# Zeros for the pooled keys made by the transposes, one-hots moved to GpSimd, and unread matmuls at the start

## The chip, the cores and the metric

One core of a Trainium2 chip runs the whole kernel. The metric is the device time of one execution in microseconds (us). Ten runs of the kernel before had a median of 254.6 us, from 253.77 to 255.77. The profile comes from one further execution.

## What is computed

Two stages follow each other. The first is attention with pooled keys and values: 8 batches of 8 heads, 576 positions, 64 dims. The mean over 8 neighbouring positions turns k and v into 72 pooled rows per head. The second routes each of the 4608 tokens (512 wide) through one of 8 experts, chosen by an input `domain_id`.

```python
k_p = k.reshape(B, H, Sp, pool, D).mean(axis=3)          # pool = 8, Sp = 72
v_p = v.reshape(B, H, Sp, pool, D).mean(axis=3)
scores = scale * np.matmul(q, k_p.transpose(0, 1, 3, 2))
attn = softmax(scores)
x = np.matmul(attn, v_p)                                  # -> (4608, 512)
for e in range(E):                                        # 8 experts
    mask = domain_id == e
    out[mask] = np.maximum(x[mask] @ w1[e], 0.0) @ w2[e]
```

All inputs are float32 in HBM. The kernel works in float16 and accumulates in float32.

## The kernel before

**Order.** The instruction order of every engine is written out by hand: the code issues instructions engine by engine in the order in which its functions are called (`tc.manual_schedule()`), and a list `plan` of (due time, unit) pairs, sorted by due time, says in which order the units of the attention stage are called. The due times are only an order, not microseconds. Each engine then works its instructions off in that order and waits where data or a buffer is missing.

**Loads.** Attention works on pairs of batches, `pr` = 0 to 3. For each pair, `load_pair` (line L108) brings k, q and v into SBUF, each with one transfer of 1152 KB as float16 (pair 0's q in two parts). All of them are issued by GpSimd and go, converted from float32 on the way, through one DMA queue (q0 of the profile) in the order of issue: k, q, v of pair 0, then of pair 1, 2, 3, then the first expert's w1. The tiles have two buffers each, so a load of pair 2 is issued once pair 0's tile is read, and so on.

**Head.** While the first k is loaded, VectorE zeroes four tiles (L118: the two gather buffers `xg`; L123: the two `kz` tiles), then builds index constants and, with a few small matmuls (L175, L183, L187), the expert number of each token. `rank_mm` (L216) and `rank_post` (L223 to L248) count tokens per expert, `slot_post` and `perm_prep` turn this into a slot per token.

**Pooled keys.** `kp_units(pr)` pools k: 16 matmuls with an identity (L424), accumulated in PSUM and copied to `kps`. Then `turn` transposes each of the 9 groups of `kps` into two halves of partitions (L432). The halves are copied (L417 on VectorE, L415 on ScalarE) into `kz`, where partitions 0 to 63 hold the keys for even positions and partitions 64 to 127 those for odd positions. The other half of each stays at the zeros written once at the start, so that a score matmul over 128 partitions (L507) picks one parity.

**The rest of a pair.** `qt_units` transposes q (L489, L491, L493), `vp_units` pools v (L455 to L476), `sc_unit` makes scores and their exponentials (L507, L509), `av_unit` multiplies with v and divides (L526 to L531) into `x_sb`. Three `av_unit`s fill a tile of 384 KB that `x_write` (L545) sends to the DRAM tensor `x_lin` on the queue of SyncE (q1 of the profile). `x_rows` holds the writes of pairs 0 and 1 back behind a one-row transfer `gate` (L550) that reads the last v tile, so none of them starts before the last v has landed. There are 12 such writes, nine for pairs 0 to 2.

**One-hots.** `perm_units(pr)` builds, for the 9 token columns of a pair, the one-hot rows `op` of the slot's low 7 bits (L345 on VectorE, three columns at a time), `eq` of its block (L352 on VectorE), and `vc` from `eq` (L359 on GpSimd). `perm_mm` (L371) multiplies them on TensorE. The result is the list of rows that each expert gathers.

**Experts.** After the writes of pairs 0 to 2, GpSimd gathers rows of `x_lin` by indirect DMA (L589), first three blocks for expert 0, then w2 of expert 0 (tag `q`, L583), three blocks for expert 1, and w1 and w2 of expert 1 (tags `v`, `k`). TensorE transposes the gathered rows (L603), makes the hidden layer (L639) and the output (L655). Results leave by indirect DMA (L664).

Of the kernel before, what the change touches and what calls it, by code (L numbers as in the profile page):

```python
# [7 lines left out]
F32 = mybir.dt.float32  # L8
F16 = mybir.dt.float16
I32 = mybir.dt.int32  # L10
AFT = mybir.ActivationFunctionType
# [10 lines left out]
NC_ = 9  # L22
# [17 lines left out]
def kernel(  # L40
# [27 lines left out]
    def wide():  # L68
        return ps.tile([128, 8, 128], F32, tag="wide", bufs=1, name="wide")
# [41 lines left out]
    with tc.manual_schedule():  # L111
# [2 lines left out]
        nc.sync.dma_start(dom64[:], moe_domain_id.bitcast(I32).rearrange(  # L114
            "(p s two) -> p s two", p=64, two=2))
        xg = [per.tile([128, NBL, HD], F16, name="xg%d" % i) for i in range(2)]
        for t in xg:
            nc.vector.memzero(t[:].rearrange("p j d -> p (j d)"))  # L118
        kt, vt, qt_ = {}, {}, {}

        kz = [wk.tile([128, 2, 16, 72], F16, tag="kz", bufs=2, name="kz") for i in range(2)]
        for t in kz:
            nc.vector.memzero(t[:].rearrange("p a b c -> p (a b c)"))  # L123
        kt[0] = load_pair(k, 0, "k")
        qt_[0] = load_pair(q, 0, "q", (0, 48, 72))

# [15 lines left out]

        iota_f = rt.tile([128, 128], F32, name="iota_f")
        nc.vector.tensor_copy(iota_f[:], iota_row[:])
        iota_h = const.tile([128, 128], F16, name="iota_h")
        nc.vector.tensor_copy(iota_h[:], iota_row[:])
        col_f = const.tile([128, 1], F32, name="col_f")
        nc.vector.tensor_copy(col_f[:], iota_col[:])
        ident = const.tile([128, 128], F16, name="ident")
# [31 lines left out]
        for cc in range(NC_):  # L181
            if cc <= 4:
                nc.tensor.matmul(Rv[:, :, cc, :], selA[:, 128 * cc:128 * cc + 128], domT[:, :, 0, :],  # L183
                                 start=True, stop=(cc < 4), skip_group_check=True)
            if cc >= 4:
                c0 = 128 * (cc - 4)
                nc.tensor.matmul(Rv[:, :, cc, :], selB[:, c0:c0 + 128], domT[:, :, 1, :],  # L187
                                 start=(cc > 4), stop=True, skip_group_check=True)
        g_i = rt.tile([128, 1], I32, name="g_i")
        nc.vector.tensor_scalar(out=g_i[:], in0=iota_col[:], scalar1=7, scalar2=None,  # L190
                                op0=ALU.bitwise_and)
# [14 lines left out]
        blk_h = blk_i = c0 = gap = mrow = mt = nblk_f = nblk_i = nov_f = od = ork = orun = ovf = ovf_h = pos_h = pos_i = rank = rk = run_ = slot_i = slotf = tmp = None  # L206
# [5 lines left out]
        def rank_mm():  # L212
            nonlocal rk
            rk = small(), small()
            for t, w in zip(rk, (Lm, ones)):
                nc.tensor.matmul(t[:, 0:E * NCH], w[:], oh[:].rearrange("p e c -> p (e c)"),  # L216
                                 start=True, stop=True)
# [75 lines left out]
            return v.units  # L293

        def perm_prep():
            nonlocal blk_h, blk_i, pos_h, pos_i
# [7 lines left out]
            pos_h = const.tile([128, NCH], F16, name="pos_h")  # L304
            nc.vector.tensor_copy(pos_h[:], pos_i[:])
            blk_h = const.tile([128, NCH], F16, name="blk_h")
            nc.vector.tensor_copy(blk_h[:], blk_i[:])

        def token_of(pool, row, n, v=nc.vector):

# [26 lines left out]
        def perm_units(pr):  # L337
            cs = slice(NC_ * pr, NC_ * pr + NC_)
            box = {}

            def op(i):
                if i == 0:
                    box["op"] = rt.tile([128, NC_, 128], F16, tag="op", bufs=2, name="op")
                c0 = NC_ * pr + 3 * i
                nc.vector.tensor_tensor(box["op"][:, 3 * i:3 * i + 3, :],  # L345
                                        iota_h[:].unsqueeze(1).to_broadcast([128, 3, 128]),
                                        pos_h[:, c0:c0 + 3].unsqueeze(2).to_broadcast([128, 3, 128]),
                                        op=ALU.is_equal)

            def pick():  # L350
                eq = rt.tile([128, NC_, NBLK], F16, tag="eq", bufs=2, name="eq")
                nc.vector.tensor_tensor(eq[:], iota_h[:, 0:NBLK].unsqueeze(1).to_broadcast([128, NC_, NBLK]),  # L352
                                        blk_h[:, cs].unsqueeze(2).to_broadcast([128, NC_, NBLK]),
                                        op=ALU.is_equal)
# [50 lines left out]
        def kp_units(pr):  # L405
            s = st.setdefault(pr, {})
            kk = kt[pr][:].rearrange("p (w t) d -> p t w d", t=8)
            kps = wk.tile([128, 9, D], F16, tag="kps", bufs=1, name="kps")
            kpT = kz[pr % 2]
            s["kpT"] = kpT  # L410
            box = {}

            def evac(dst, src, act):
                if act:
                    nc.scalar.activation(dst, src, AFT.Copy)  # L415
                else:
                    nc.vector.tensor_copy(dst, src)  # L417

            def pool(w0, w1, t0):
                if t0 == 0:  # L420
                    box[w0] = small()
                pv = box[w0][:, 0:64 * (w1 - w0)].rearrange("p (w d) -> p w d", d=64)
                for t in range(t0, t0 + 4):
                    nc.tensor.matmul(pv, ident[:], kk[:, t, w0:w1, :], start=(t == 0), stop=(t == 7))  # L424
# [267 lines left out]
        for pr in range(NP):  # L692
            t0 = 16.0 * pr
            for h in range(16):
                plan.append((t0 + h, -1, lambda pr=pr, h=h: sc_unit(pr, h)))

            if pr + 1 < NP:
                at = [8.6 + 1.78 * j for j in range(NC_)]
                if pr == NP - 2:
                    at[4:] = [16.1, 17.1, 18.2, 19.3, 20.4]  # L700
            else:
                at = [9.2, 10.7, 12.2, 13.7, 16.0, 16.4, 17.0, 17.6, 18.2]
            for j in range(NC_):
                plan.append((t0 + at[j], len(plan), lambda pr=pr, j=j: av_unit(pr, j)))
            k0, k1 = (2.6, 6.6) if pr < NP - 1 else (0.5, 6.5)
            put([lambda pr=pr, i=i: run(vp_units_(pr, i)) for i in range(11)], t0 + k0, t0 + k1)
            if pr + 1 < NP:
                put([lambda pr=pr, i=i: run(kp_units_(pr + 1, i)) for i in range(6)], t0 + 7.5, t0 + 11.0)
# [197 lines left out]
```

## Time and profile before

| | us |
|---|---|
| median of 10 runs | 254.6 |
| lowest and highest of them | 253.77, 255.77 |
| the profiled execution: its time | 256.01 |
| the profiled execution: its span, first to last instruction | 254.3 |
| TensorE busy in the span | 220.3 (87%) |
| VectorE busy | 126.5 (50%) |
| ScalarE busy | 94.4 (37%) |
| GpSimd busy | 117.2 (46%) |
| mean granted TensorE clock | 0.981 |

"PE" is TensorE's matmuls, "PEld" its weight loads, "DVE" VectorE, "ACT" ScalarE, "POOL" GpSimd, "SP" SyncE. A name like L424 is the line of the kernel before. The time between the span and the execution's time, 1.7 us here, lies outside of the first and last instruction. All positions such as "at 80.43" are microseconds from the span's start.

### The profile page before, as it was taken

To read this page: it belongs to the slowest core of one execution; us is meant where nothing else is said; L and a number is where in the kernel's file an instruction comes from. 1 tells how busy PE (TensorE), PEld (TensorE's weight loads), DVE (VectorE), ACT (ScalarE), POOL (GpSimd) and SP (SyncE) were. 2 spreads that over 40 slices of the span, in tenths; PEclk is the share of its full clock that TensorE was granted. 3 is DMA by queue.
4 is the path that set the end of the run, shared out by engine and by line. 5 is a ranking of instruction groups with operands and counts; after the bars stand their busy time and mean duration, and the time that the engine had idled before them with its cause. 6 is when DMAs were issued, how large, how long until landed. Compare 5 with 4: busy or idle time off the path is not lost.

```text
span 254.3 us, 4896 instructions
## 1 busy us (share of the span) xinstructions
PE 220.3 (87%) x1979; PEld 145.9 (57%) x1979; DVE 126.5 (50%) x283; ACT 94.4 (37%) x159; POOL 117.2 (46%) x157
## 2 busy tenths in 40 slices
PE   0287779999987769799989999999999999999990
PEld 0156667777766445445645755756755656656640
DVE  7856889686779752233242433332343332343320
ACT  2037777888785805122311321312302312303210
POOL 8000613130000382276856776676676767653042
PEclk9999999999999968999999999999999999999997
DMA  6999999999999279998989979969969969942032
GB/s 107 207 222 210 223 216 212 220 216 211 215 254 409 89 156 239 238 276 169 182 255 147 253 205 151 245 208 163 248 210 177 249 178 206 248 170 106 1 113 91
DMA packets 21372, 50.20 MB, mean 197 GB/s; under 512 B 2334, under 2 KB 10592, under 8 KB 19938
## 3 DMA queue, kind: packets, MB, share of 16 engines
q0 software_dynamic: 19536, 45.10, 83.1%
q1 hardware_dynamic: 1810, 4.76, 4.8%
q8 instruction: 16, 0.26, 0.4%
q14 instruction: 10, 0.08, 0.1%
HBM read 67.15 MB, written 15.20 MB: 324 GB/s over the span
## 4 chain that ended last, share of the span: by engine, by line
PE 53%; DVE 13%; issue 10%; DMA 9%; ACT 7%; POOL 5%; POOLq 1%; DVEq 0%; ACTq 0%
PE big L639 16%; PE small L655 14%; DMA v<-in_moe_w_dram 6%; PE wide L639 6%; PE wide L655 3%; ACT at L509 3%; DVE x_sb L531 3%; PE small L424 3%; POOL out_dram L664 3%; PE turn L603 3%; DVE qT L493 2%; DMA x_lin<-x_sb 2%; PE small L489 2%; PE big L507 2%; POOL xg L589 2%
## 5 line engine op out<-in xcount | busy, mean ns | idle before, releaser
L589 POOL DMA_INDIRECT xg<-x_lin,xrow x40 | 41.5, 1038 | 48.5 <-DVE tok L100 33.4
L664 POOL DMA_INDIRECT out_dram<-y,tok x40 | 40.2, 1006 | 44.9 <-DVE y L660 19.4
L655 PEld LDWEIGHTS <-hT 128*128 128x128 f16 x272 | 25.9, 98 | 26.6
L645 DVE TENSOR_SCALAR hT<-big 128x640 f16<-128x640 f32 (+1 forms) x24 | 17.4, 725 | 33.4 <-PE big L639 23.9
L509 ACT ACTIVATE at<-big 72x576 f16<-72x576 f32 x45 | 28.3, 646 | 8.4 <-PE big L507 7.3
L662 ACT ACTIVATE y<-small 128x512 f32<-128x512 f32 x16 | 9.6, 597 | 50.2 <-PE small L655 48.0
L643 ACT ACTIVATE hT<-big 128x640 f16<-128x640 f32 (+1 forms) x24 | 15.0, 623 | 31.7 <-PE big L639 31.7
L660 DVE COPY y<-small 128x512 f32<-128x512 f32 x16 | 11.1, 691 | 29.6 <-PE small L655 26.5
L639 PEld LDWEIGHTS <-v 128*128 128x128 f16 x192 | 18.7, 98 | 10.3 <-issue 1.8
L639 PEld LDWEIGHTS <-k 128*128 128x128 f16 x192 | 19.1, 100 | 8.9 <-issue 1.7
L639 PE MATMUL big<-xT,v 128*128 128x320 f16 (+2 forms) x144 | 21.8, 299 | 1.5 <-DVE hT L645 0.9
L604 DVE COPY xT<-turn 128x1024 f16<-128x1024 f16 (+1 forms) x24 | 14.3, 598 | 16.8 <-PE turn L603 13.8
L639 PE MATMUL big<-xT,k 128*128 128x320 f16 (+2 forms) x140 | 21.9, 307 | 0.0
L507 PE MATMUL big<-qT,kz 128*72 128x288 f16 x90 | 18.3, 287 | 2.5 <-DVE qT L493 1.1
L655 PE MATMUL small<-q,hT 128*128 128x512 f16 x80 | 18.6, 379 | 0.0
L655 PE MATMUL small<-k,hT 128*128 128x512 f16 x80 | 18.4, 379 | 0.0
L526 PEld LDWEIGHTS <-at 72*128 72x128 f16 (+1 forms) x320 | 14.8, 104 | 5.9 <-issue 2.6
L531 DVE TENSOR_TENSOR x_sb<-big,rcp 128x512 f16<-128x512 f32 x22 | 15.2, 692 | 0.8
L639 PEld LDWEIGHTS <-q 128*128 128x128 f16 x128 | 12.5, 98 | 5.2
L603 PEld LDWEIGHTS <-xg 128*128 128x128 f16 x160 | 10.9, 99 | 7.8 <-DMA xg<-x_lin,xrow 2.3
L603 PE MATMUL turn<-ident,xg 128*128 128x128 f16 x160 | 13.7, 224 | 1.8 <-DMA xg<-x_lin,xrow 1.6
L655 PE MATMUL small<-v,hT 128*128 128x512 f16 x64 | 14.8, 379 | 0.0
(152 smaller groups left out, 336.4 us busy)
## 6 DMA issues: line engine op xcount, KB each, us to landing
k<-in_moe_w_dram POOLq DMA_DIRECT2D x6, 1024.0 KB
q<-in_moe_w_dram POOLq DMA_DIRECT2D x5, 1024.0 KB
v<-in_moe_w_dram POOLq DMA_DIRECT2D x5, 1024.0 KB
k<-in_k_dram POOLq DMA_DIRECT2D x4, 1152.0 KB
v<-in_v_dram POOLq DMA_DIRECT2D x4, 1152.0 KB
x_lin<-x_sb SPq DMA_DIRECT2D x12, 384.0 KB, 6.9
q<-in_q_dram POOLq DMA_DIRECT2D x3, 1152.0 KB
q<-in_q_dram POOLq DMA_DIRECT2D x1, 768.0 KB
```

The lines of the kernel that those rows point to most:

```text
L507: nc.tensor.matmul(p[0:72, par, 0:288], s["kpT"][:, par, bh, :], s["qT"][:, :, 8 * bh:8 * bh + 8], start=True, stop=True)
L509: nc.scalar.activation(at[0:72, bh % 8, :].rearrange("p (a c) -> p a c", a=2), p[0:72, :, 0:288], AFT.Exp, scale=1.0 / 64.0)
L526: nc.tensor.matmul(pv[r0:r0 + z - a, h, 0:65], s["at", bt][0:72, h, a:z], s["vp"][0:72, 8 * bt + h, :], start=True, stop=True, skip_group_ ...
L531: nc.vector.tensor_tensor(out=x_sb.rearrange("p (h d) -> p h d", d=D), in0=pv[:, :, 0:64], in1=rcp[:].unsqueeze(2).to_broadcast([128, 8, D ...
L589: i = nc.gpsimd.indirect_dma_start(out=xg[e % 2][:, j, :], out_offset=None, in_=x_lin[0:rows, :], in_offset=bass.IndirectOffsetOnAxis(ap=x ...
L603: nc.tensor.transpose(p[:, j - a, kk, :], xg[e % 2][:, j, 128 * kk:128 * kk + 128], ident[:])
L604: nc.vector.tensor_copy(xts[e][:, :, 128 * a:128 * z].rearrange("p k (j c) -> p j k c", c=128), p[:, 0:z - a])
L639: nc.tensor.matmul(p[:, a, 0:m], w1[:, kk, 128 * fi:128 * fi + 128], xT[:, kk, s0 + m * a:s0 + m * a + m], start=(kk == 0), stop=(kk == 3))
L643: nc.scalar.activation(dst, p[:, 0:nh, 0:m], AFT.Relu)
L645: nc.vector.tensor_scalar(out=dst, in0=p[:, 0:nh, 0:m], scalar1=0.0, scalar2=None, op0=ALU.max)
L655: nc.tensor.matmul(p, hT[:, fi, 128 * j:128 * j + 128], w2[:, fi, :], start=(fi == 0), stop=(fi == 7))
L664: i = nc.gpsimd.indirect_dma_start(out=out, out_offset=bass.IndirectOffsetOnAxis(ap=orig[0][:, bl:bl + 1], axis=0), in_=y[:], in_offset=No ...
```

## The change

- Only the first gather buffer is still zeroed by VectorE. ScalarE copies those zeros into the second one, and into `kps`, which is now one permanent tile with 64 zero columns on either side of the pooled keys.
- `turn` transposes 128 columns of `kps` at a time, the keys and 64 zeros before or behind them. The zero rows of `kz` therefore come out of the transposes, and all 128 partitions are copied at once: three copies per pair (groups 0 to 3, 4 to 7, 8), on VectorE except for one of pair 0 on ScalarE. `kz` is no longer zeroed beforehand.
- The one-hots `op` are built on GpSimd, one column per instruction, 36 instructions in all. `eq` reads float32 instead of float16.
- `warm(n)` issues n matmuls of 512 columns on zeros, whose result nobody reads: 6 before the first transposes, 4 after the small matmuls, 3 after `rank_mm`.

In the changed kernel GpSimd's queue holds, behind the load of q of pair 2: 9 `op`, 2 `vc`, 9 `op`, load v of pair 2, 2 `vc`, 6 `op`, load k of pair 3, 3 `op`, 2 `vc`, load q of pair 3, 9 `op`, load v of pair 3, 2 `vc`, load w1 of expert 0, and then the gathers.

```diff
-        for t in xg:
-            nc.vector.memzero(t[:].rearrange("p j d -> p (j d)"))
+        kps = rt.tile([128, NC_, 3 * D], F16, name="kps")
+        zero = xg[0][:].rearrange("p j d -> p (j d)")
+        nc.vector.memzero(zero)
+        nc.scalar.activation(kps[:].rearrange("p w d -> p (w d)"), zero[:, 0:NC_ * 3 * D], AFT.Copy)
+        nc.scalar.activation(xg[1][:].rearrange("p j d -> p (j d)"), zero, AFT.Copy)
+        def warm(n):
+            p = wide()
+            for i in range(n):
+                nc.tensor.matmul(p[:].rearrange("p a b -> p (a b)")[:, 0:512], zero[:, 0:128], zero[:, 0:512],
+                                 start=True, stop=True, skip_group_check=True)
+        warm(6)
-        kz = [wk.tile([128, 2, 16, 72], F16, tag="kz", bufs=2, name="kz") for i in range(2)]
-        for t in kz:
-            nc.vector.memzero(t[:].rearrange("p a b c -> p (a b c)"))
...
-        iota_h = const.tile([128, 128], F16, name="iota_h")
-        nc.vector.tensor_copy(iota_h[:], iota_row[:])
...
+        warm(4)                      # after the small matmuls of L183 and L187
...
-                nc.vector.tensor_tensor(box["op"][:, 3 * i:3 * i + 3, :],
-                                        iota_h[:].unsqueeze(1).to_broadcast([128, 3, 128]),
-                                        pos_h[:, c0:c0 + 3].unsqueeze(2).to_broadcast([128, 3, 128]),
-                                        op=ALU.is_equal)
+                for c in range(3):
+                    nc.gpsimd.tensor_scalar(out=box["op"][:, 3 * i + c, :], in0=iota_f[:],
+                                            scalar1=pos_f[:, c0 + c:c0 + c + 1], scalar2=None, op0=ALU.is_equal)
...
-            kpT = kz[pr % 2]
+            kpT = wk.tile([128, 2, 16, 72], F16, tag="kz", bufs=2, name="kz")
...
-                    evac(kps[:, w0:w1, :], pv, pr == 0)
+                    evac(kps[:, w0:w1, D:2 * D], pv, pr == 0)
...
-                    for half in range(2):
-                        nc.tensor.transpose(p[64 * half:64 * half + 64, w - w0, :], kps[:, w, :], ident[:])
-                for i, act in ((0, False), (1, True)):
-                    q = slice(64 * i, 64 * i + 64)
-                    evac(kpT[q, i].rearrange("p b (w g) -> p w b g", g=8)[:, w0:w1],
-                         p[q, 0:w1 - w0, :].rearrange("p w (b g) -> p w b g", g=8), act)
+                    for par in range(2):
+                        a = D - D * par
+                        nc.tensor.transpose(p[:, 2 * (w - w0) + par, :], kps[:, w, a:a + 2 * D], ident[:])
+                evac(kpT[:].rearrange("p a b (w g) -> p w (a b) g", g=8)[:, w0:w1],
+                     p[:, 0:2 * (w1 - w0), :].rearrange("p (w a) (b g) -> p w (a b) g", a=2, g=8),
+                     pr == 0 and w0 == 4)
...
-                    + [lambda: turn(0, 5), lambda: turn(5, 9)])
+                    + [lambda: turn(0, 4), lambda: turn(4, 8), lambda: turn(8, 9)])
...
         rank_mm()
+        warm(3)
```

More of the change, by code (lines that the diff above doesn't have):

```diff
@@ L205 @@
                                 op=ALU.is_equal)
-        blk_h = blk_i = c0 = gap = mrow = mt = nblk_f = nblk_i = nov_f = od = ork = orun = ovf = ovf_h = pos_h = pos_i = rank = rk = run_ = slot_i = slotf = tmp = None
+        blk_f = blk_i = c0 = gap = mrow = mt = nblk_f = nblk_i = nov_f = od = ork = orun = ovf = ovf_h = pos_f = pos_i = rank = rk = run_ = slot_i = slotf = tmp = None
         thl = const.tile([128, 2, NCH], F16, name="thl")
@@ L295, in perm_prep @@
         def perm_prep():
-            nonlocal blk_h, blk_i, pos_h, pos_i
+            nonlocal blk_f, blk_i, pos_f, pos_i
             pos_i = rt.tile([128, NCH], I32, name="pos_i")
@@ L303, in perm_prep @@
                                     op0=ALU.logical_shift_right)
[L304 to L307, printed above, removed]
+            pos_f = rt.tile([128, NCH], F32, name="pos_f")
+            nc.vector.tensor_copy(pos_f[:], pos_i[:])
+            blk_f = rt.tile([128, NCH], F32, name="blk_f")
+            nc.vector.tensor_copy(blk_f[:], blk_i[:])
         def token_of(pool, row, n, v=nc.vector):
@@ L344, in op @@
                 c0 = NC_ * pr + 3 * i
-                nc.vector.tensor_tensor(box["op"][:, 3 * i:3 * i + 3, :],
-                                        iota_h[:].unsqueeze(1).to_broadcast([128, 3, 128]),
-                                        pos_h[:, c0:c0 + 3].unsqueeze(2).to_broadcast([128, 3, 128]),
-                                        op=ALU.is_equal)
+                for c in range(3):
+                    nc.gpsimd.tensor_scalar(out=box["op"][:, 3 * i + c, :], in0=iota_f[:],
+                                            scalar1=pos_f[:, c0 + c:c0 + c + 1], scalar2=None, op0=ALU.is_equal)
             def pick():
                 eq = rt.tile([128, NC_, NBLK], F16, tag="eq", bufs=2, name="eq")
-                nc.vector.tensor_tensor(eq[:], iota_h[:, 0:NBLK].unsqueeze(1).to_broadcast([128, NC_, NBLK]),
-                                        blk_h[:, cs].unsqueeze(2).to_broadcast([128, NC_, NBLK]),
+                nc.vector.tensor_tensor(eq[:], iota_f[:, 0:NBLK].unsqueeze(1).to_broadcast([128, NC_, NBLK]),
+                                        blk_f[:, cs].unsqueeze(2).to_broadcast([128, NC_, NBLK]),
                                         op=ALU.is_equal)
@@ L407, in kp_units @@
             kk = kt[pr][:].rearrange("p (w t) d -> p t w d", t=8)
-            kps = wk.tile([128, 9, D], F16, tag="kps", bufs=1, name="kps")
-            kpT = kz[pr % 2]
+            kpT = wk.tile([128, 2, 16, 72], F16, tag="kz", bufs=2, name="kz")
             s["kpT"] = kpT
@@ L707 @@
             if pr + 1 < NP:
-                put([lambda pr=pr, i=i: run(kp_units_(pr + 1, i)) for i in range(6)], t0 + 7.5, t0 + 11.0)
+                put([lambda pr=pr, i=i: run(kp_units_(pr + 1, i)) for i in range(7)], t0 + 7.5, t0 + 11.0)
                 put([lambda pr=pr, i=i: run(qt_units_(pr + 1, i)) for i in range(5)], t0 + 11.6, t0 + 15.2)
```

## The prediction

> **What bounds the kernel now.** I read the page's slices first, then the busy time by stretch, then the chain of waits. DMA is busy from the first slice to the thirteenth, while TensorE's clock falls in the two slices about 90 us. By stretch (columns: PE, PEld, DVE, ACT, POOL busy us, granted clock, DMA share, GB/s):
>
> ```profile
> 6.00:12.00 6.00, 1.33 (x13) 0.83 (x14) 5.08 (x23) 0.00 (x0) 0.77 (x2) 1.00 1.01 209
> 42.00:48.00 6.00, 5.57 (x91) 4.75 (x89) 4.24 (x11) 5.49 (x12) 0.54 (x1) 1.00 1.02 215
> 66.00:72.00 6.00, 5.65 (x86) 4.62 (x84) 5.16 (x16) 4.34 (x7) 0.00 (x0) 1.00 1.01 203
> ```
>
> ```profile
> 78.00:80.00 2.00, 1.62 (x27) 1.36 (x25) 1.93 (x7) 1.09 (x2) 0.00 (x0) 1.00 1.03 412
> 80.00:82.00 2.00, 0.93 (x19) 0.74 (x17) 1.51 (x6) 0.65 (x1) 0.00 (x0) 1.00 1.04 409
> 82.00:84.00 2.00, 1.75 (x25) 1.29 (x24) 1.63 (x5) 1.90 (x4) 0.00 (x0) 1.00 0.72 286
> 84.00:86.00 2.00, 1.38 (x16) 0.90 (x15) 1.70 (x4) 1.71 (x4) 0.00 (x0) 1.00 0.05 19
> ```
>
> The DMA share is 1.0 in all of them until 82: the engines have no gap in which work could start sooner. Next the SyncE queue's waits and the chain of waits:
>
> ```profile
> SPq L550 <- DMA v<-in_v_dram: 70.0, 1, 70.0
> ```
>
> ```profile
> 79.71 0.70 DVE x_sb L531
> 80.42 0.02 issue
> 80.43 4.86 DMA x_lin<-x_sb
> ...
> 87.69 3.46 DMA xg<-x_lin,xrow
> ...
> 94.97 14.67 DMA v<-in_moe_w_dram
> 109.63 0.05 issue
> 109.68 1.47 PE big L639 x8
> ```
>
> The chain names VectorE's `x_sb` as the releaser of the ninth write at 80.43. That reading misleads. The first nine writes wait for the gate, the gate for the last v, and it goes at 71.44. Nine writes of 393 KB are 3.54 MB, at 410 GB/s 8.6 us of saturated DMA, behind 1.05 MB of w1. The write of 80.43 lands 4.86 us later because others stand before it: the trace's completion counts put the eighth write's landing at 84.35 and the ninth's at 85.29, the same 0.94 us apart as the six before them. So two limits nearly meet here, and the one that decides is DMA: twelve loads of 1.18 MB at 213 GB/s from 3 us to 71.4, w1, nine writes to 85.3. Then GpSimd issues the gathers at 86.30, q (w2 of expert 0) at 90.03 and v (w1 of expert 1) at 94.97, and v lands at 109.63. From there TensorE is busy 89.79 of the 90 us between 130 and 220, and the rest follows: 254.3 - 109.7 = 144.6 us that the change does not touch. Before v lands, TensorE waits 1.52 us for q (until 103.09) and 0.58 us for v.
>
> **The change, part by part.** The sum is made against the profiled span of 254.3 us, whose execution took 256.0. The median of the runs, 254.6, is 1.4 below that, so I carry differences over to the median. A difference under 0.3% (0.8 us) cannot be told from none here.
>
> Zeros. VectorE starts its index work at 6.00, after four memsets. Without three of them (2.55 to 6.09) the next one, L144, waits for GpSimd's iota, done at 3.32 + 0.29 = 3.61. It moves 2.35 us earlier, and dropping `iota_h` adds 0.2 at most. On ScalarE two copies of 1728 and 2560 elements come in; the nearest row, a 1024-element copy of 1.02 us (L491), gives 1.7 + 2.6 = 4.3 us, from 2.33 to 6.6. ScalarE has nothing to do until 14.51 (it waited 12.36 us). With that cover gone, they would delay the pooled keys by their length.
>
> Unread matmuls. The first pooling takes 3.95 us for 16 matmuls, the last pair's 0.59 + 0.54 + 0.44 + 0.44 = 2.01 on the chain:
>
> ```profile
> 12.18 3.95 PE small L424 x16
> ...
> 64.38 0.59 PE small L424 x4
> 65.22 0.54 PE small L424 x4
> 66.02 0.44 PE small L424 x4
> 66.71 0.44 PE small L424 x4
> ```
>
> A clock already up is worth between 0 and 1.94 us; I take 1. The 13 matmuls cost 0.22 us each (eight of 512 columns in 1.73 at L655) to 0.43 at half speed: 2.6 + 1.7 + 1.3 us. They lie in waits of 2.33 to 5.4 for `domf`, 6.5 to 8.35 for `oh`, and about 9 to 10.1 for k, with some 0.2 us too much in the last at half speed.
>
> The Trainium skill ("TensorE: Matmul & The Clock Gate", The HAM clock gate) says that the clock is half until a free-running window of about 3.4 us was busy, and half again after an idle one. By it the 13 matmuls, spread over 8 us, lift the clock in some phases of that window and not in others; the head would gain 1.9 us or nothing, and the end of the sum the same either way. The profile agrees in kind: half clock from 91 to 97.9, twice 3.4 us.
>
> Turning. The 18 transposes stay 18 (224 ns each at L432, 218 for the full width at L489: no change). VectorE's two copies of 0.48 + 0.41 us become 1024, 1024 and 256 elements. By slope of these two rows (0.56 ns per element, 0.12 fixed) that is 0.70 + 0.70 + 0.26 = 1.66, +0.77 per pair. ScalarE sheds 0.70 + 0.59 = 1.29 per pair. Both copies of a half came one behind the other (ACT waited for DVE's), so a turn gets some 0.5 us shorter.
>
> One-hots. VectorE loses 12 instructions of 645 ns, 7.4 us busy; `eq` on float32 stays near 0.52 (an f32 tensor-tensor of 288 elements takes 0.458). GpSimd gains 36. No row shows this operation. Bounds: 0.18 (copy of one element, L614) and 0.85 (`vc`, two inputs, 360 elements); nearest is the 128x128 iota at 0.29, so I take 0.35, 12.6 us in all. Behind them in GpSimd's queue stand the loads of v2, k3, q3, v3 and w1, issued at 28.46, 32.06, 39.50, 45.72 and 52.11. Their turn on the saturated queue comes only when the load before them has landed, at about 48, 53, 59, 64 and 70: 18 us of cover or more, against 12.6 (or 30.6 at the upper bound, of which 21 us fall into GpSimd's idle time between 21 and 50). Who could wait is TensorE at `perm_mm(0)`, 28.57 now: slots are ready near 21.5, plus 9 x 0.35 and two `vc` of 0.85 is 26.4, about when TensorE gets there. At 0.85 each it is 31, a stall of some 4 us.
>
> The Trainium skill ("GPSIMD Engine Reference", Performance versus the Vector engine) speaks against this move: elementwise work is about twice as slow there, on SBUF ports shared with VectorE. By it three instructions would cost 1.3 us for VectorE's 0.65, which is 15 us in all and still under cover. Two `vc` at 26.42 took 2.09 us and later 1.53, so sharing may show here too.
>
> How far it carries. The head gains 2.35 + 1 + 0.5, near 4 us. But q0 lands fully at 15.66, v0 at 21.11 (its first use is at 22.80), k1 at 27.69 (first use 29.05). So by k1 only 1.4 us are left, and with VectorE relieved by 7.4 - 2.3 = 5.1 us it can grow back to the 3.8 us between v3's landing (71.42) and its first use (75.21). Then the ninth write is issued 1.4 to 3.8 us earlier, and stands in the same queue behind the same 3.14 MB. Its gain is between 0 and 0.4 us (the 0.28 share missing in 82 to 84); I take 0.2. The tenth write (87.36) moves out of the way of the gathers, which brings transposes forward, but not q or v. Sum: 0.2 us faster, 254.4.
>
> **Rivals.**
> *The advance carries through* (faster). If the write queue has gaps, or a write issued earlier lands earlier, the gathers move with `x_sb`: -1.4, up to -2.4 us with VectorE's relief: 253.2 (252.2). For it stands that the chain itself runs through `x_sb`; against it, the share of 1.03 and the even 0.94 us between landings.
> *The clock falls again before q lands* (slower). TensorE has even less to do from 84 to 93, and if expert 0's hidden layer ends earlier, its 1.52 us wait at 101.57 grows. In this profile 3.4 us with TensorE 0.46 busy (87.6 to 91.0) led to half clock; the 3.4 us around 103 were 0.56 busy and did not. From a wait near 2.2 us on it could. One such 3.4 us stretch costs 1.7 of dense work, less the 0.58 us before v: +1.1, 255.7; two cost +2.8.
> *GpSimd is dear* (slower). From about 0.6 us per one-hot on, `perm_mm` stalls TensorE by more than the 1.4 to 2 us advance, and the ninth write is late: at 0.85, some +2, 256.6.
> *The unread matmuls lift no clock*: the head gains 3 instead of 4 us, and the time is the forecast's.
>
> **How the numbers follow.** The forecast (DMA paces it, 253.9 to 255.2) gets 0.58, with 0.08 of it below and 0.03 above what can be told; the advance 0.25; the clock 0.11; GpSimd 0.06. That is faster 0.33, same 0.47, slower 0.20. The range reaches into the advance and the clock's case, 252.6 to 255.8; the forecast's own range is 253.9 to 255.2.
>
> **What would show it.** Right: L424's first pooling starts near 10.1 and first scores near 18.5 instead of 22; the gate still goes at 71.4; `x_sb`'s ninth write is issued before 79.1 and lands at 85 to 85.5; first gather near 86.2, v's landing near 109.5. Wrong: a first gather before 85.3, or v's landing moved by over 0.8 us. GpSimd's one-hots should show 0.25 to 0.5 us each.

## The result and the profile after

The changed kernel takes 259.27 us (median of 9 runs, 258.43 to 260.96) where the kernel before took 254.58 (31 runs, 253.77 to 255.9): 1.0194 times as long [1.0174, 1.0214], 4.7 us more. Forecast was 254.4 with a range up to 255.8. Ratios here are formed from undisturbed runs alone and need not equal the quotient of two medians. The profiled execution of the changed kernel took 261.85 us, its span is 260.1. In the profiles after, line numbers have moved: one-hots L353, `vc` L365, `perm_mm` L377, pooling L430, scores L513, `x_sb` L537, writes L551, gate L556, gathers L595, transposes of gathered rows L609, hidden layer L645.

From the page of the changed kernel, busy times and then the granted clock in 40 slices of 6.5 us:

```profile
PE 229.9 (88%) x1992; PEld 152.7 (59%) x1992; DVE 119.9 (46%) x270; ACT 94.9 (36%) x154; POOL 138.7 (53%) x193
...
PEclk9999898599999985899999999999999999999999
```

GpSimd is busy 21.5 us longer than before, VectorE 6.6 us shorter. The clock, which before fell only near 95, now falls around 32 and from 44 to 51 too. The table by stretch (same columns as in the prediction):

```profile
6.00:12.00 6.00, 5.27 (x25) 2.46 (x26) 5.03 (x18) 0.22 (x1) 1.50 (x2) 1.00 1.00 208
42.00:48.00 6.00, 4.27 (x49) 3.55 (x45) 2.55 (x7) 2.42 (x5) 5.96 (x10) 0.66 1.05 221
66.00:72.00 6.00, 5.57 (x90) 4.73 (x88) 3.65 (x14) 5.42 (x12) 0.00 (x0) 1.00 1.02 207
78.00:80.00 2.00, 1.60 (x26) 1.35 (x24) 1.97 (x6) 1.88 (x4) 0.00 (x0) 1.00 1.04 408
80.00:82.00 2.00, 1.30 (x24) 1.02 (x24) 1.03 (x5) 0.93 (x2) 0.00 (x0) 1.00 0.74 298
82.00:84.00 2.00, 2.00 (x39) 1.91 (x38) 1.93 (x6) 1.29 (x2) 0.00 (x0) 1.00 0.07 28
84.00:86.00 2.00, 1.62 (x33) 1.40 (x30) 1.97 (x6) 1.29 (x2) 0.00 (x0) 1.00 0.55 205
86.00:88.00 2.00, 0.93 (x14) 0.73 (x15) 1.70 (x6) 0.65 (x1) 0.00 (x0) 1.00 0.20 78
```

Loads run as before, up to 72. From 82 to 88 the DMA engines are busy for only 0.07 to 0.55 of the time: the write queue, which paced the kernel before, now waits for data. From 42 to 48 GpSimd is busy 5.96 of 6 us and TensorE only 4.27, at a clock of 0.66. The waits of TensorE between 18 and 112 us begin with:

```profile
PE small L377 <- POOL vc L365: 5.9, 3, 3.6
```

and the group of the one-hots is, first in the kernel before (its groups by line between 6 and 90 us), then in the changed one (the page's costliest groups):

```profile
L345 DVE TENSOR_TENSOR op<-iota_h,pos_h 128x384 f16<-128x384 f16 x12 | 7.4, 645 | 0.0
L353 POOL TENSOR_SCALAR op<-iota_f,pos_f 128x128 f16<-128x128 f32 x36 | 21.4, 609 | 2.6 <-DVE blk_f L314 2.5
```

`perm_mm` waits 5.9 us in three pieces for `vc`, which stands behind the one-hots in GpSimd's queue. One one-hot takes 0.59 us (median; mean 0.609). The chain of waits, in its first part, shows how the first wait comes about:

```profile
22.13 0.18 DVE pos_i L306
22.63 5.05 POOL op L353 x9
27.68 0.51 issue
28.20 1.53 POOL vc L365 x2
29.73 1.37 POOL op L353 x3
...
43.78 0.79 POOL vc L365
44.61 0.76 PE small L377 x9
```

The slots are ready at 22.63, nine one-hots and two `vc` later it is 29.73, and then TensorE can go on. Between the two parts shown the chain stays on GpSimd: its queue of one-hots, `vc` and issues of loads decides when the third `perm_mm` starts, at 44.61 (40.60 before). Later in the chain, where the kernel before had x_lin, xg and v:

```profile
94.83 0.70 DVE x_sb L537
95.53 0.04 issue
95.58 0.89 PE wide L532 x16
96.47 0.97 PE turn L609 x8
...
100.32 0.42 DVE xT L610
100.75 0.04 issue
100.79 1.44 PE wide L645 x4
...
112.97 1.73 PE small L661 x8
114.69 1.30 PE big L645 x8
```

No transfer is left in it. The first gather goes at 90.21 (86.30 before) and v lands, by the trace's completion counts, at 113.10 (109.63 before), but TensorE first multiplies with v at 114.53 and waits for neither q nor v nor the gathered rows. It is late by itself, with the end of the attention stage. Before, it waited 1.6 us for gathered rows, 1.5 for q and 0.6 for v. These are its waits between 85 and 130 us, for before and, the longest one alone, for after:

```profile
PE turn L603 <- DMA xg<-x_lin,xrow: 1.6, 2, 1.4
PE small L655 <- DMA q<-in_moe_w_dram: 1.5, 1, 1.5
...
PE big L639 <- DMA v<-in_moe_w_dram: 0.6, 1, 0.6
```

```profile
PE wide L645 <- DVE xT L610: 2.0, 1, 2.0
```

The first product with v moves from 109.68 to 114.53, by 4.85 us; the span of the profiled execution grows by 5.8, the median of the runs by 4.7. The transfers are late too: v lands only 1.4 us before TensorE reaches it, so a TensorE on time would have waited for v until 113.10.

### The profile page after: what moved, and what is told of

The parts are those of the page before. It is cut to its first block, busy times and chain, and to the rows that moved or that the text cites. A ratio compares the mean times of both kernels' runs of the same rounds, so it can differ in the third digit from the quotient of the medians.

```text
span 260.1 us, 4951 instructions
## 1 busy us (share of the span) xinstructions
PE 229.9 (88%) x1992; PEld 152.7 (59%) x1992; DVE 119.9 (46%) x270; ACT 94.9 (36%) x154; POOL 138.7 (53%) x193
## 4 chain that ended last, share of the span: by engine, by line
PE 59%; POOL 12%; DVE 12%; issue 11%; ACT 3%; another core or an unknown queue 1%; POOLq 1%; ACTq 0%
PE big L645 16%; PE small L661 15%; PE wide L645 6%; POOL op L353 6%; PE wide L661 4%; PE turn L609 3%; POOL out_dram L670 3%; DVE x_sb L537 3%; PE big L513 2%; PE small L430 2%; DVE qT L499 2%; ACT at L515 2%; PE big L532 2%; POOL vc L365 1%; PE small L461 1%
## 5 line engine op out<-in xcount | busy, mean ns | idle before, releaser
L670 POOL DMA_INDIRECT out_dram<-y,tok x40 | 40.2, 1006 | 47.7 <-DVE y L666 20.5
L595 POOL DMA_INDIRECT xg<-x_lin,xrow x40 | 41.5, 1038 | 44.9 <-ACT at L515 30.7
L661 PEld LDWEIGHTS <-hT 128*128 128x128 f16 x272 | 25.8, 98 | 26.7
L645 PEld LDWEIGHTS <-k 128*128 128x128 f16 x192 | 19.1, 101 | 10.5 <-issue 3.3
L645 PEld LDWEIGHTS <-v 128*128 128x128 f16 x192 | 18.8, 98 | 9.4 <-issue 1.6
L353 POOL TENSOR_SCALAR op<-iota_f,pos_f 128x128 f16<-128x128 f32 x36 | 21.4, 609 | 2.6 <-DVE blk_f L314 2.5
L645 PE MATMUL big<-xT,v 128*128 128x320 f16 (+2 forms) x144 | 21.8, 299 | 0.9 <-DVE hT L651 0.9
L645 PE MATMUL big<-xT,k 128*128 128x320 f16 (+2 forms) x140 | 22.2, 309 | 0.0
L513 PE MATMUL big<-qT,kz 128*72 128x288 f16 x90 | 19.3, 301 | 2.8 <-DVE qT L499 1.3
L532 PEld LDWEIGHTS <-at 72*128 72x128 f16 (+1 forms) x320 | 15.8, 110 | 6.6 <-DVE x_sb L537 2.9
L645 PEld LDWEIGHTS <-q 128*128 128x128 f16 x128 | 12.5, 98 | 5.2
L537 DVE TENSOR_TENSOR x_sb<-big,rcp 128x512 f16<-128x512 f32 x22 | 15.2, 691 | 0.8
L515 ACT ACTIVATE at<-wide 72x576 f16<-72x576 f32 x19 | 12.2, 643 | 9.1 <-PE wide L513 9.0
```

The lines of the kernel that those rows point to most:

```text
L353: nc.gpsimd.tensor_scalar(out=box["op"][:, 3 * i + c, :], in0=iota_f[:], scalar1=pos_f[:, c0 + c:c0 + c + 1], scalar2=None, op0=ALU.is_equal)
L513: nc.tensor.matmul(p[0:72, par, 0:288], s["kpT"][:, par, bh, :], s["qT"][:, :, 8 * bh:8 * bh + 8], start=True, stop=True)
L515: nc.scalar.activation(at[0:72, bh % 8, :].rearrange("p (a c) -> p a c", a=2), p[0:72, :, 0:288], AFT.Exp, scale=1.0 / 64.0)
L532: nc.tensor.matmul(pv[r0:r0 + z - a, h, 0:65], s["at", bt][0:72, h, a:z], s["vp"][0:72, 8 * bt + h, :], start=True, stop=True, skip_group_ ...
L537: nc.vector.tensor_tensor(out=x_sb.rearrange("p (h d) -> p h d", d=D), in0=pv[:, :, 0:64], in1=rcp[:].unsqueeze(2).to_broadcast([128, 8, D ...
L595: i = nc.gpsimd.indirect_dma_start(out=xg[e % 2][:, j, :], out_offset=None, in_=x_lin[0:rows, :], in_offset=bass.IndirectOffsetOnAxis(ap=x ...
```

## The experiments

The theory after this reading: GpSimd's price per one-hot makes TensorE wait at `perm_mm`; the waits let the clock fall; both make the attention stage late by more than the transfers' waits can take up. Rivals: GpSimd's work slows its neighbours (VectorE, the loads issued behind it); the new turns or the unread matmuls cost something; the half clock at the end costs it.

| kernel | first scores of pair 3 | ninth write issued, landed | first gather | first product with v | time to before |
|---|---|---|---|---|---|
| before | 74.33 | 80.43, 85.29 | 86.30 | 109.68 | 1 |
| after | 80.70 | 86.80, 89.11 | 90.21 | 114.53 | 1.0194 |
| e1, one-hots on VectorE | 76.11 | 82.20, 85.56 | 86.66 | 109.57 | 0.9991 |
| e2, GpSimd's one-hots alone | 81.29 | 87.39, 89.70 | 90.72 | 115.55 | 1.0232 |
| e3, `perm_mm` later | 75.89 | 81.98, 85.57 | 86.68 | 108.79 | 1.0032 |
| e4, unread matmuls in the waits | 78.45 | 84.54, 86.85 | 87.95 | 111.63 | 1.0103 |
| e7, unread matmuls alone | 73.18 | 79.28, 85.27 | 86.28 | 107.86 | 0.9964, 1.0007 |
| e8, turns and zeros alone | 73.84 | 79.94, 85.59 | 86.69 | 109.10 | 0.9994 |
| e9, one-hots in halves | 87.13 | 93.23, 95.54 | 96.64 | 120.79 | one run |

Positions are of the profiled executions, landings from the trace's completion counts.

**e1: the one-hots go back to VectorE, all else as after** (with them, `iota_h` comes back and `eq` reads float16 again).

```diff
-                for c in range(3):
-                    nc.gpsimd.tensor_scalar(out=box["op"][:, 3 * i + c, :], in0=iota_f[:],
-                                            scalar1=pos_f[:, c0 + c:c0 + c + 1], scalar2=None, op0=ALU.is_equal)
+                nc.vector.tensor_tensor(box["op"][:, 3 * i:3 * i + 3, :],
+                                        iota_h[:].unsqueeze(1).to_broadcast([128, 3, 128]),
+                                        pos_h[:, c0:c0 + 3].unsqueeze(2).to_broadcast([128, 3, 128]),
+                                        op=ALU.is_equal)
```

> The changed kernel with only the one-hots back on VectorE (float16, three columns per instruction). Theory 1, GpSimd's one-hots at 0.6 us each make TensorE wait at the three perm_mm and the ninth write late: with them gone the head's 1.9 us (first scores at 20.2 instead of 22.0) stays, the ninth write is issued before 79.5, lands near 85.3 all the same, first gather near 86.3, and the time is 254.0 to 254.9, no faster than the kernel before. Theory 2, the rest of the change (three turns per pair, all copies on VectorE, zeros on ScalarE) slows the attention stage: the time stays at 257 or more. Theory 3, the advance of the head carries through to the gathers: 253.2 or less.

Measured 255.44 (10 runs), 0.9991 of before [0.9956, 1.0025]. The loss is gone: it belongs to the one-hots. What was expected of the ninth write missed: it was issued at 82.20, later than before, although the first scores came 2.3 us earlier (19.73). The lead was lost up to the second pooling (29.02 against 28.88), TensorE waited 1.2 us for v of pair 0, and its clock fell three times (8.7 to 12.1, 22.3 to 25.8, 36.0 to 39.4). The time did not mind, since the write landed at 85.56, where the queue let it. Nor did half clock from 90.6 to 100.9, 10.3 us as in after, cost anything here: the rival of the clock at the end falls with it.

**e2: only the one-hots move to GpSimd, all else as before** (with them, `iota_h` goes and `eq` reads float32).

```diff
-                nc.vector.tensor_tensor(box["op"][:, 3 * i:3 * i + 3, :], ...
+                for c in range(3):
+                    nc.gpsimd.tensor_scalar(out=box["op"][:, 3 * i + c, :], in0=iota_f[:],
+                                            scalar1=pos_f[:, c0 + c:c0 + c + 1], scalar2=None, op0=ALU.is_equal)
```

> The kernel before with only the one-hots moved to GpSimd. Theory 1: TensorE waits some 2 to 6 us at perm_mm in all, the ninth write is issued after 83, the first gather after 88.5: 257 to 260. Slots are ready some 2 us later than in the changed kernel, but TensorE gets there later too. Theory 2: within 0.5 us of the kernel before, 254.1 to 255.1.

Measured 261.18 (4 runs), 1.0232 [1.0174, 1.0291], at least the whole loss and more than the 257 to 260 expected. The first two waits of TensorE in the list from 18 to 112 us:

```profile
PE small L368 <- POOL vc L356: 4.9, 3, 3.6
PE small L652 <- DMA q<-in_moe_w_dram: 3.1, 1, 3.1
```

Three waits at `perm_mm` again. Here the late gathers (90.72) show as a wait for q, which after did not have: the two ways to be late lie close together. The granted clock is full from 49.7 to 107.8 here, so the loss does not need the half clock that after has from 95.

**e3: after, with `perm_mm` of the first three pairs placed later in the written order**, 3.2 to 4.7 steps of `plan`. GpSimd's work stays as it is.

```diff
-            put([lambda i=i: perm_mm(i)], k1 + 2.3, k1 + 2.3)
+            kp = k1 + (5.5, 6.0, 7.0, 2.3)[i]
+            put([lambda i=i: perm_mm(i)], kp, kp)
```

> The changed kernel with perm_mm of pairs 0, 1 and 2 due later (10.5, 15 and 21.5 instead of 7.3, 11.3 and 16.8), so that GpSimd has made the one-hots by then; the one-hots stay on GpSimd. Theory 1: no wait at perm_mm of over 0.5 us, ninth write before 80, first gather near 86.3, 254.0 to 255.0. Rival, GpSimd's work itself slows the others (its 21 us beside VectorE's copies, or the loads behind it in its queue): the waits vanish, but the gathers stay after 88 and the time over 257.

Measured 256.06 (10 runs), 1.0032 [0.9992, 1.0072]. The one-hots' group on the page:

```profile
L353 POOL TENSOR_SCALAR op<-iota_f,pos_f 128x128 f16<-128x128 f32 x36 | 21.7, 622 | 2.6 <-DVE blk_f L314 2.5
```

and TensorE's longest waits from 18 to 60 us:

```profile
PE small L495 <- DVE qT L499: 1.6, 1, 1.6
PE small L461 <- DMA v<-in_v_dram: 0.9, 1, 0.9
```

GpSimd works as long (21.7 us for 21.4), beside the same neighbours and ahead of the same loads, and the loss is gone or nearly so. What cost time was the place at which TensorE stood and waited, not the 21 us. Even without these waits the kernel is not faster than before, and both expectations were missed: the time, 254.0 to 255.0, and the ninth write, before 80, which was issued at 81.98.

**e4: after, with unread matmuls where TensorE waits**, 16 ahead of the first `perm_mm` and 8 ahead of the third. They shorten no wait; they keep TensorE busy in it.

```diff
+            if pr in (0, 2):
+                warm((16, 0, 8)[pr])
```

> The changed kernel with 16 unread matmuls ahead of perm_mm of pair 0 and 8 ahead of that of pair 2, which fill most of TensorE's waits there and keep its clock up; the waits stay. Theory 1a, the waits themselves make the ninth write late: the half clock of 30.3 to 33.7 and 43.9 to 50.8 goes, yet the time falls by 1 us at most, to 258 or more. Theory 1b, the half clock that follows the waits costs most of it (10.2 us at half speed, up to 5 us of matmuls): the ninth write is issued 2 us earlier or more, and the time falls to 256 to 257.

Measured 258.98 (8 runs, 256.25 to 262.67), 1.0103 [1.0059, 1.0147], against 1.0194 for after. TensorE's timeline at the first place, and then the clock by stretch, for after and for e4:

```profile
27.69 3.62 PE L128 MATMUL wide<-xg 128*128 128x512 f16 x16
31.14 0.49 PE L379 MATMUL small<-vc,op 128*128 128x80 f16 x9
```

```profile
26.90:30.30 3.40, 0.52 (x11) 0.48 (x11) 0.00 (x0) 0.36 (x1) 3.40 (x7) 1.00 1.03 217
30.30:33.70 3.40, 3.40 (x22) 2.31 (x21) 1.57 (x5) 0.65 (x1) 3.40 (x7) 0.50 1.02 214
...
40.50:43.90 3.40, 2.17 (x32) 1.49 (x29) 2.88 (x7) 2.10 (x4) 3.36 (x7) 1.00 1.04 219
43.90:47.30 3.40, 2.69 (x27) 2.33 (x27) 1.13 (x3) 1.13 (x2) 3.35 (x6) 0.51 1.02 217
```

```profile
30.30:33.70 3.40, 3.40 (x38) 2.55 (x37) 1.30 (x4) 0.65 (x1) 3.40 (x6) 1.00 1.02 214
43.90:47.30 3.40, 3.40 (x46) 2.50 (x45) 1.14 (x3) 1.56 (x3) 3.35 (x7) 1.00 1.04 219
```

In after, 3.4 us with 0.52 busy are followed by 3.4 us at half clock; in e4 the same stretch runs at full clock, with 38 matmuls instead of 22. The unread matmuls lasted longer than the waits: the `vc` for the first and the third `perm_mm` were done at 28.56 and 43.47, and these started at 31.14 and 44.97 (29.78 and 44.61 in after). All the same, the scores of pair 3 and the ninth write come 2.3 us earlier than in after. From the third `perm_mm` to the first scores of pair 3 it takes 33.5 to 33.8 us where the clock is full (before, e1, e4, e7, e8), 35.0 with 3.4 us at half clock (e2), and 36.1 and 35.9 with 6.8 us (after, e9). So at least 2.3 of the 6.4 us by which after is late there are half clock, and about half of the loss in time went with them. The rest is the third `perm_mm` itself, which starts 4.0 us later than in the kernel before. The ninth write came where theory 1b had it, the time where theory 1a had it (258 or more).

**e5 and e6: before, with the load of w1 of expert 0 held back**, to test what the write queue is worth: a small copy on GpSimd reads one of pair 2's `x_sb` columns (the sixth in e5, the ninth in e6) ahead of the load.

```diff
-        put(wload_units(0, 0, 1), 32.0, 32.0)
+        w10 = wload_units(0, 0, 1)[0]
+        def after_x():
+            nc.gpsimd.tensor_copy(mark[:], st[2]["x"][0:1, 2, 0:1])
+            w10()
+        put([after_x], 49.5, 49.5)          # e6: 52.5
```

> The kernel before, with the load of expert 0's w1 held back on GpSimd by a one-element copy that waits for column 5 of pair 2's x_sb (near 76.5 us), so that its 1.05 MB of DMA no longer stand in front of the nine writes. Nothing else is changed. Theory 1, DMA paces the way to the gathers: the writes have the queue to themselves from 71.5, the ninth (issued near 80.4) lands near 83 instead of 85.3, the first gather goes at 83.5 to 84.5, q and v land 2 to 4 us earlier, and the time is 251.5 to 253.5. Rival, the chain's own reading, x_sb decides when the ninth write lands: the first gather stays near 86.3, and the time at 254.3 to 255.5, or later if w1 now comes late for expert 0's hidden layer (near 93.8).

e5 measured 258.76 (4 runs), 1.0107 [1.0019, 1.0196], where a gain was expected. GpSimd's timeline:

```profile
77.98 0.81 POOL L583 DMA_DIRECT2D k<-in_moe_w_dram  x1 [0.33 <-PE big L507]
90.05 1.08 POOL L589 DMA_INDIRECT xg<-x_lin,xrow  x1 [11.26 <-DMA x_lin<-x_sb]
```

The eighth write landed 2.4 us earlier (81.98 for 84.35), but w1, issued at 77.98, shares the engines with the ninth write of 80.66, which now needed until 89.12. TensorE's first product with v moved to 112.63, 2.95 us. With the attention stage unmoved (first scores of pair 3 at 74.56), a ninth write that lands late is enough to lose the time.

> As the run before it, but the copy waits for column 8 of pair 2 (near 80.4), so that w1 starts only when the ninth write is issued. Theory 1: ninth write lands near 82.8, first gather near 84, w1 lands near 89, the gathers' data stand behind it in the queue; 251.5 to 253.5, at most 0.5 us from the run before it. Rival (x_sb decides): 254.3 or more.

e6 measured 254.25, 0.9971 [0.993, 1.0011]. The ninth write landed at 84.40 and the first gather went at 85.32, 1.0 us earlier than before: the floor moves with what stands in the queue, by 1.0 and not by 2. w1 itself now landed at 90.16, with the gathers' rows behind it.

**e7 and e12: before, with the 13 unread matmuls alone**, in their three places (`warm` as in the change); the same kernel twice.

```diff
+        warm(6)
...
+        warm(4)
...
+        warm(3)
```

> The kernel before with only the 13 unread matmuls. The four memsets stay, so the waits into which they fall are there too. DMA paces: first pooling takes 2 to 3.5 us instead of 3.95, and the time is within 0.5 us of the kernel before. Rival, a clock lifted early falls later and costs matmuls in the attention stage: ninth write after 82, but up to 82.5 or so it lands at 85.3 to 85.6 all the same.

> The kernel before with only the 13 unread matmuls once more, in five rounds. In three rounds it took 0.9964 of the kernel before, interval 0.9931 to 0.9997, while its first gather came no earlier. If that gain is real it shows again below 1.000: 0.994 to 0.998. If it was the spread of the runs, the ratio lies within 0.999 to 1.002.

Measured 254.17, 0.9964 [0.9931, 0.9997], and again 255.37, 1.0007 [0.9975, 1.0038]: no gain that repeats. The first pooling took 2.55 us in place of 3.95, and the ninth write was issued 1.15 us earlier; its landing (85.27) and the first gather (86.28) did not move. In e12's profile the attention stage was 2.0 us later than in e7's (first scores of pair 3 at 75.22 for 73.18), and the first gather went at 86.17: an advance or a lag of this size does not reach it. Between the two profiles lies a stretch at half clock from 35.2 to 38.6, which e12 has and e7 has not.

**e8: zeros and turns alone**: after, with the one-hots on VectorE as in e1 and no unread matmuls.

```diff
-        warm(6)
...
-        warm(4)
...
-        warm(3)
...     # and the one-hots as in e1
```

> The changed kernel with the one-hots back on VectorE and without the unread matmuls: what is left is the zero columns of kps, the three turns per pair and the zeros on ScalarE. DMA paces: 254.3 to 255.6, within 0.5 us of the kernel before. The ninth write shows whether the turns cost the attention stage anything: before 80.5 if they cost nothing (the head starts 2.35 us earlier), near 82 if the three copies on VectorE (+0.77 us per pair) eat that.

Measured 255.16, 0.9994 [0.9957, 1.0032]: these parts cost nothing and bring nothing. The clock stayed up from 15.7 to 90.8.

**e9: after, with each one-hot in two halves of 64 columns**, 72 instructions, to see what an instruction costs and whether the loss grows with it.

```diff
-                for c in range(3):
-                    nc.gpsimd.tensor_scalar(out=box["op"][:, 3 * i + c, :], in0=iota_f[:], ...
+                for c in range(6):
+                    h = slice(64 * (c % 2), 64 * (c % 2) + 64)
+                    nc.gpsimd.tensor_scalar(out=box["op"][:, 3 * i + c // 2, h], in0=iota_f[:, h], ...
```

> The changed kernel with each one-hot instruction split into two of 64 columns (72 instead of 36). Now one takes 0.59 us. If that is mostly a fixed cost per instruction (the 128x128 iota takes 0.30, a copy of one element 0.18), each half takes 0.4 or more, 29 us in all, the waits at perm_mm grow by 3 us or more and the time passes 262. If it goes by elements (4.4 ns each), a half takes 0.3 to 0.35 and the time stays within 1.5 us of the changed kernel.

The tile `op`, with minimum, median and maximum in ns:

```profile
L354 POOL TENSOR_SCALAR op<-iota_f,pos_f x72: 431/433/810, 22.3 to 58.8; 128x64 f16<-128x64 f32 x72
```

Half the columns take 433 ns where all 128 took 591: (591 - 433) / 64 = 2.5 ns per element and 275 ns that do not depend on the size. TensorE waits 11.8 us for `vc` (5.9 in after), and the profiled execution took 268.33 us, 6.5 more than that of after, for 9.2 us more of one-hots (30.6 for 21.4). About two thirds of what GpSimd works longer reach the end.

**e10 and e11: before, with w1 of expert 0 in two halves**, the second held back as in e6; e10 with the 13 unread matmuls as well.

```diff
-        put(wload_units(0, 0, 1), 32.0, 32.0)
+        w10 = wload_units(0, 0, 2)
+        def after_x():
+            nc.gpsimd.tensor_copy(mark[:], st[2]["x"][0:1, 2, 0:1])
+            w10[1]()
+        put([w10[0]], 32.0, 32.0)
+        put([after_x], 52.5, 52.5)
```

> The kernel before with the 13 unread matmuls and with expert 0's w1 loaded in two halves, the first where it is now, the second behind the one-element copy that waits for column 8 of pair 2. DMA paces: eighth write lands near 83 instead of 84.35, the ninth, issued near 79.3, near 83.5 to 84, first gather at 84.5 to 85 instead of 86.3, v lands 1 to 2.5 us earlier: 252.3 to 253.8, 0.990 to 0.996 of the kernel before. Rival: what counts lies behind the gathers (the chain of q and v on the queue), the gathers move by 1.5 us and v by less than 0.5: 254.3 or more.

> As the run before it, without the unread matmuls: the ninth write is issued near 80.5. DMA paces: first gather at 84.5 to 85.3, 253.0 to 254.5. If the gain of the run before it came from the unread matmuls alone, this one is within 0.3 us of the kernel before.

e10 measured 254.42 (12 runs), 0.9967 [0.9936, 0.9999]; e11 255.12 (12 runs), 1.0004 [0.9974, 1.0033]. First gathers went at 84.97 and 85.11, 1.2 to 1.3 us earlier than before. TensorE then no longer waited for v, but reached it only at 108.91 and 108.62, 0.8 and 1.1 us earlier: it had its own work until then. So the gathers moved as expected and the expected times (252.3 to 253.8 and 253.0 to 254.5) were missed. Why even the 1.1 us do not show in e11's time is not settled, and no version tried is clearly faster than the kernel before.

## Why the prediction was wrong

**The step that failed: the price of a one-hot.** The working took 0.35 us, between 0.18 and 0.85, from the nearest row, the 128x128 iota of 0.29. It was 0.59 (e9 gives its two parts). An iota reads nothing; the one-hot reads float32 and a scalar per partition; that this makes the difference is not shown. Everything from there follows the forecast's own sum: slots at 22.63 (21.5 forecast) plus 5.05 for nine one-hots (3.15), 0.51 between, and 1.53 for `vc` (1.7) is 29.72 in place of 26.4, while TensorE stood ready at 29.78 - 3.64 = 26.14. Of these 3.3 us the price is 1.9, the later slots are 1.1. GpSimd's own elementwise work would have been nearer, but not near enough: `vc` with 360 elements at 0.85 is 2.4 ns per element with no fixed part, where the measured slope is 2.5, and a line through it and the copy of one element (0.18) puts a one-hot at 0.42, an estimate. The fixed part of 275 ns could be read from no row of the kernel before.

The Trainium skill ("GPSIMD Engine Reference", Performance versus the Vector engine) was cited with about twice VectorE's time, which gave the estimate of 1.3 us for three columns. The runs show 3 x 0.591 = 1.77 us against VectorE's mean of 0.645, 2.7 times: the rule pointed the right way and fell short, and the 0.43 per one-hot of that estimate was still nearer than the 0.35 taken.

**The rival that came true was priced too low.** "GpSimd is dear" put the point of decision at about 0.6 us per one-hot, which is what was measured, and the loss at 0.85 at 2 us; at 0.59 it was 4.7. Two things were left out. Only the first `perm_mm` was looked at, but GpSimd stays behind through 50 us, and TensorE waits at three (3.64, 0.73 and 1.55 us). And the clock fell after such waits. The three waits are not to be added up: as long as GpSimd's queue decides, time lost or gained ahead of a `perm_mm` only changes the length of the wait there. What counts is the third one, at 44.61 in place of 40.60, 4.0 us late by GpSimd's queue. From it to the first scores of pair 3 it took 36.1 us in place of 33.7, the 2.4 us of half clock that e4 shows. Together this is the 6.4 by which those scores are late. At the first product with v 4.85 of it are left; the rest fits the waits for gathered rows, q and v (3.7 us before) that TensorE no longer has.

**The way it reached the end** was also another one. "GpSimd is dear" had a late ninth write, and by it late gathers and a late v. These came (v at 113.10, 3.5 us late), but TensorE, with the rest of pair 3 and half clock from 95.1 to 105.4, was later still. What follows the first product with v kept its length within 1 us: 145.6 us in the profile for 144.6.

**The clock rival** looked for the fall behind the attention stage, near 103. The half clock there did grow, from 6.8 to 10.2 us, but e1 has the same 10.2 without a loss; the falls that cost time were those behind the waits at `perm_mm`. The rival used 0.46 busy as a stretch that lowers the clock and 0.56 as one that does not. Here 2.17 of 3.40 us, 0.64, ahead of 43.9 were followed by half clock, so 0.56 is no safe line. In the traces the granted clock changes in steps of 3.41 us. Of the steps at full clock up to 130 us, in all fourteen profiles, those with TensorE busy for at most half of the step were all followed by half clock, those busy for more than 0.68 never, and between 0.53 and 0.68 both happened: 0.53 kept the clock in e9 (1.82 of 3.41 us from 39.90), 0.68 lost it in e3 (2.34 of 3.42 us from 87.96).

The Trainium skill ("TensorE: Matmul & The Clock Gate", The HAM clock gate) has half clock after an idle window. The row of 0.52 of 3.40 us fits that loosely, the row of 2.17 does not: the records show a fall after a stretch that is far from idle.

**What held.** The write queue as the floor is the best supported part: e7, e12, e8, e1, e3 and before issue the ninth write anywhere from 79.28 to 82.20 and it lands at 85.16 to 85.59, the first gather at 86.17 to 86.69. Past that, issues at 84.54 and later land 2.31 us after them (e4, after, e2, e9), which puts the corner near 83.2, an estimate. "The advance carries through" is refuted by e7. The gate: its wait on the SyncE queue is 70.1 long, as it was 70.0:

```profile
SPq L556 <- DMA v<-in_v_dram: 70.1, 1, 70.1
```

The loads behind the one-hots stayed hidden (v of pair 3 landed at 71.55 for 71.42). ScalarE's two copies took 1.64 + 2.32 = 3.96 us (4.3 forecast) under cover. Copies of 1024 elements out of the turns took 0.69 to 0.70 (0.70) and of 256 0.28 (0.26). First scores came at 20.18, 1.8 us earlier than before; 18.5 had been forecast. Of the 1.7 us between, 0.7 are the start of the pooling, at 10.81 in place of 10.1, since the last three unread matmuls ran until 11.01 with k there at 10.21. The pooling took 3.31 us in place of 2.95, and from its end to the scores it took 6.1 where 5.4 were forecast (5.9 before): the turn got no shorter.

**What was wrong without cost:** that the advance grows back with VectorE relieved, so that the ninth write is issued 1.4 to 3.8 us earlier. In e3, with VectorE relieved and no wait of TensorE for `vc`, it was issued at 81.98, 1.55 us later than before; TensorE waited 1.6 us for `qT` and 0.9 for v of pair 0 there, and its clock was half from 40.2 to 43.6. In e1, with the one-hots on VectorE, the advance shrank below zero as well, up to the second pooling, at v of pair 0 and in three stretches of half clock; e8, which is e1 without the unread matmuls, kept full clock and issued it at 79.94. The floor hid all of this.

**Open:** the profiled executions differ by 5.8 us, as their spans do, the medians by 4.7; one wait of VectorE in after (2.53 us at 119.19) has no releaser that the profile names. Whether e3's 0.3% is a loss is not told by its interval.

## What to carry to other kernels

Before work is moved to an idle engine, write down who waits for its last product and when, for every repetition and not for the first alone; the idle share of the engine says nothing about that. Price a new instruction by a row of the same engine doing the same kind of reading, with a fixed part and a part per element, and, where no row has both, let the upper bound decide where a consumer stands close behind. A wait put into a dense TensorE stage can cost more than its length, since the clock may fall after it (here 2.4 us for 6.8 us at half clock); where the producer cannot be faster, placing the consumer later in the written order (e3) removes nearly the whole loss.

## What the runs showed of the hardware

- GpSimd's comparison with a scalar per partition, float32 to float16: 591 ns for 128 elements per partition, 433 for 64, that is 275 ns fixed and 2.5 ns per element.
- The clock fell to half after a stretch of 3.4 us in which TensorE was busy for 2.17 us by the records. In e4, where unread matmuls filled the waits, it was full from 24.5 to 92.7.
- From the third `perm_mm` to the first scores of pair 3 the same work took 33.5 to 33.8 us at full clock, 35.0 with 3.4 us at half clock (e2) and 36.1 with 6.8 (after).
- Two queues share the engines at a price for the later one: with 1.05 MB issued 2.7 us ahead of it on GpSimd's queue and the write before it still under way, a write of 393 KB on SyncE's queue took 8.5 us to land (e5); with nothing ahead it took 2.31 (after).
- One kernel's attention stage can differ by 2 us from profile to profile, with a stretch of half clock in one and not in the other, and the first gather at 86.28 and 86.17 all the same (e7 and e12).
